# Input rows and result rows of an S4 block with an MLP: one transfer of 128 partitions, or four of 32

## The chip, the cores and the metric

The kernel runs on one core of a Trainium2 chip. The metric is the device time of one execution, in microseconds (us). A core has a matrix engine (TensorE, "PE" in the profile), a vector engine (DVE), a scalar engine (ACT), GpSimd (POOL) and SyncE (SP), which in this kernel only issues transfers. Each engine works through its own instructions strictly in order. The transfers themselves (DMAs) run on 16 DMA engines that all queues share.

## The reference, cut to what matters

2048 tokens of 512 channels, all in float32. The block is a layer norm with a scale and a shift from a conditioning vector, a long convolution over the tokens (S4), a residual addition, a second layer norm, an MLP with Mish, and a second residual addition.

```python
x = A_u                                    # (1, 2048, 512)
mod = (silu(c) @ w_mod)...                 # sa, ca, ga, sb, cb, gb
h = layernorm(x) * (1 + ca) + sa
x = x + ga * S4(h)                         # K from exp(dt*A*l), then FFT convolution, + h * Dskip
h = layernorm(x) * (1 + cb) + sb
x = x + gb * (mish(h @ w1 + b1) @ w2)      # w1 512 x 1792, w2 1792 x 512
```

## The kernel before

**Layout of the tokens.** A token number is split as 64·p + 16·a + j, with p from 0 to 31, a from 0 to 3 and j from 0 to 15. A tile of input rows holds on partition 32·a + p, for one or several j, the 512 channels of the token: four groups of 32 partitions, one for each a. In DRAM a step in p is 64 rows, a step in a is 16 rows, and n successive j are n successive rows, so that a partition's share is one stretch of n · 2 KB. The result tiles of the MLP (`ot`) have the same layout with one j.

**The head.** The first transfers on SP's queue are small parameters (`ldt`, `raw`, `ident`, `cT`, `dtap`, `hl`), then the input rows: five calls of `x_rows` in line 630 load all 2048 rows (4 MB) into the tiles `xr` in the order j = 12 to 15, 4 to 7, 8 and 9, 10 and 11, 0 to 3. Behind them on the same queue come the constants `bdk`, `bdu`, `di`, `b1`, the 2 MB table `mf` (line 694), the first four tiles of the conditioning weights `wm` (line 433), and the 2 MB table `mi` (line 698). On GpSimd's queue `sel`, `mc`, `ac` and `su` are loaded at the same time.

**Who uses the rows first.** `stats` takes mean and variance of each row: for j = 12 to 15 on ACT (`junk`, lines 680 and 684), for the others on DVE (`bst`, line 674). `norm` (line 498) then normalizes all 16 row tiles, and `ua` (line 505) sends them through TensorE as the first step of the convolution's transform. Meanwhile `params` prepares the exponents of the convolution kernel on DVE and ACT (`raw`, an arctangent among it, lines 281 and 291), and TensorE builds the angles (`psel`, line 307, `pang`, line 346) and the conditioning (`pmodr`, line 440, which reads `wm`). ACT, DVE and PE each have an order in which these two strands are interleaved, and a wait in one strand holds up the other.

**The middle.** Four blocks of 128 channels go through kernel generation, transform, product and inverse in a software pipeline whose order comes from the table `ORDER` and the priorities in `PRI` and `PRI0`; the framework makes the fixed order of each engine's instructions and all the waits from these. In this stage `x_rows` is called with a block number `b` (line 602): it loads 128 of the 512 channels and already makes four transfers of 32 partitions, 64 KB each. The sum of input and convolution is stored to DRAM as `x2d`.

**The MLP.** Four token tiles `tt` of 512 tokens, each with 14 blocks `f` of the hidden layer. `mm1` makes one hidden block (12 matmuls into a bank `pm`), ACT applies Mish, and `mm2`, two blocks behind, adds it to the four output banks `PO[tt][q]` (12 matmuls `po`). The six PSUM banks rotate, so that the banks of the next token tile come free when `fin_q` has read those of the last one. `fin_q` (line 895) does this for each q: DVE multiplies the bank by the gate (line 903, the step that frees the bank), adds the residual `xr` or `xf` (line 904), and SP stores the tile `ot` (line 905). `ot` has two buffers, so the multiplication for q = 2 waits until the store of q = 0 has landed, and the one for q = 3 until the store of q = 1 has. Between the stores SP's queue holds the loads of `xr` from `x2d` (line 899, four for each q).

Of the kernel before, what the change touches and what calls it, by code (L numbers as in the profile page):

```python
# [18 lines left out]
P = 128  # L19
D = 512  # L20
# [93 lines left out]
def s4_block(ctx, tc, io, out):  # L114
    nc = tc.nc
# [32 lines left out]
    def view(src, offset, ap):  # L148
        return bass.AP(tensor=src.tensor, offset=src.offset + offset, ap=ap)
# [35 lines left out]

    def x_rows(dst, j0, n, b=None):
        w = D if b is None else P
        if b is None:
            nc.sync.dma_start(dst, view(io["A_u"], j0 * D, [[16 * D, 4], [64 * D, 32], [1, n * D]]))  # L189
            return  # L190
        for a in range(4):
            nc.sync.dma_start(dst[32 * a:32 * a + 32], view(io["A_u"], (16 * a + j0) * D + b * P,
                                                            [[64 * D, 32], [D, n], [1, P]]))

    bdk = cst.tile([P, 256], F32, name="bdk")
    bdu = cst.tile([P, 64], F32, name="bdu")
# [392 lines left out]
    def s_xp(y):  # L589
        b, hf, j4 = y // 8, y % 8 // 4, y % 4  # L590
        if hf == 0:
            return
        if b < NB - 1:
            t = cv.tile([P, 4, P], F32, tag="xp", name=f"xp{b}{j4}", bufs=2)
        elif j4 == 0:
            t = LNX[0][:, b]
        else:
            if j4 == 1:
                XP[b] = sl8(f"xp{b}").rearrange("p (q j d) -> p q j d", q=4, j=4)
            t = XP[b][:, j4]  # L600
        XP[b, j4] = t
        x_rows(t, 4 * j4, 4, b)
# [23 lines left out]
    for j0, t in ((12, xr3), (4, xr01[:, 4:8]),  # L626
                  *((j, cv.tile([P, 2, D], F32, tag="x4", name=f"xr{j}", bufs=3)) for j in (8, 10)),
                  (0, xr01[:, 0:4])):
        n = t.shape[1]
        x_rows(t, j0, n)  # L630
        XR[j0:j0 + n] = [t[:, q, :] for q in range(n)]
# [263 lines left out]
    def fin_q(tt, q, x=None):  # L895
        if x is None:
            x = MW["wr"].tile([P, NB, P], F32, tag=("yt", "q1")[q % 2], name="xr", bufs=1)
            for b in range(NB):
                nc.sync.dma_start(x[:, b], x2d[b][:, 4 * tt + q, :])
        else:  # L900
            x = x[:, :, q, :]
        o = mp.tile([P, NB, P], F32, tag="ot", name="ot")
        V.tensor_mul(o.rearrange("p b d -> p (b d)"), PO[tt][q], gbb)  # L903
        V.tensor_add(o, o, x)
        nc.sync.dma_start(view(out, (4 * tt + q) * D, [[16 * D, 4], [64 * D, 32], [1, D]]),
                          o.rearrange("p b d -> p (b d)"))

    tables("mish")
    seq = [(tt, f) for tt in range(4) for f in range(FB)]
    for n, (tt, f) in enumerate(seq):  # L910
        mm1(tt, f)
        if tt == 0:
            load_w2(f)
        if tt + 1 < 4:
            if f == 7:
                ln_load(tt + 1)
            if f == 11:
                ln_stats(tt + 1, range(NB))
                ln_norm(tt + 1)
            if f == 13:  # L920
                ln_t(tt + 1)
        if n == 3:
            gb_row()
        if n >= LAG:
            pt, pf = seq[n - LAG]
            mm2(pt, pf)
            if pf == FB - 1:
                for q in range(4):
                    fin_q(pt, q)
    xl = fin_load(3)  # L930
    for q in range(4):
        for f in range(FB - LAG, FB):
            mm2(3, f, (q,))
        fin_q(3, q, xl)
# [37 lines left out]
```

## Time and profile before

| | us |
|---|---|
| median of 3 runs | 782.93 |
| lowest and highest of them | 779.67, 785.41 |
| the profiled execution's own time | 784.37 |
| its span, from the first to the last recorded event | 782.6 |
| TensorE busy in it | 663.6 (85%) |
| DVE, ACT, GpSimd busy | 432.4 (55%), 339.0 (43%), 51.7 (7%) |
| mean TensorE clock granted | 0.938 |

The busy shares are means over stages that are limited by different things. The first 80 us, in which TensorE works little, and the hand-over from one token tile to the next in the MLP are read by their own waits and from the chain that ended last. In the rows of a timeline the first number is the start, the second the duration, and a bracket at the end tells how long the engine had been idle and what released it. In the rows by windows the last two numbers are the mean busy share of the 16 DMA engines and the rate that they moved.

### The profile page before, as it was taken

How to read it: one execution, taken by the hardware profiler on the slowest of the kernel's cores; microseconds unless marked ns; L12 is line 12 of the kernel's file. 1: busy time of each engine (PE TensorE's matmuls, PEld its weight loads, DVE VectorE, ACT ScalarE, POOL GpSimd, SP SyncE). 2: the span in 40 equal slices, each digit the busy share in tenths (PEclk: the TensorE clock that was granted, in tenths of full speed). 3: DMA queues.
4: the chain of work that ended last, by engine and by line, in shares of the span. 5: the costliest groups of instructions: out<-in, count | busy, mean ns of one | idle time of the engine just before them, and what ended most of it. 6: DMA issues, size and time to landing. Idle time of an engine off the chain costs nothing.

```text
span 782.6 us, 14045 instructions
## 1 busy us (share of the span) xinstructions
PE 663.6 (85%) x5696; PEld 510.8 (65%) x5696; DVE 432.4 (55%) x900; ACT 339.0 (43%) x529; POOL 51.7 (7%) x111
## 2 busy tenths in 40 slices
PE   0427897799999999999855799997999899989991
PEld 0214355467888878888631588886888688868881
DVE  6319885597999989995742891182113311331112
ACT  2543468555787686765520542241223222322220
POOL 1000142050206020000000000000000000000000
PEclk9957789899999999999986999998999999999997
DMA  5247488653326553565866730013001210010001
GB/s 156 109 131 295 122 189 194 189 131 101 84 67 154 156 153 95 137 185 175 249 200 168 236 95 1 0 55 103 5 1 54 67 41 0 1 54 27 1 1 54
DMA packets 97228, 82.91 MB, mean 106 GB/s; under 512 B 10376, under 2 KB 78732, under 8 KB 96524
## 3 DMA queue, kind: packets, MB, share of 16 engines
q1 hardware_dynamic: 90444, 78.14, 34.6%
q0 software_dynamic: 6720, 3.87, 2.6%
q8 instruction: 45, 0.74, 0.4%
q14 instruction: 19, 0.16, 0.1%
HBM read 54.72 MB, written 25.17 MB: 102 GB/s over the span
## 4 chain that ended last, share of the span: by engine, by line
PE 69%; DMA 10%; SPq 8%; DVE 6%; ACT 4%; issue 1%; POOL 0%; DVEq 0%; ACTq 0%; POOLq 0%
PE pm L867 18%; PE po L885 17%; PE pkg L392 4%; PE pub L525 4%; PE pang L346 4%; DMA out<-ot 4%; PE pkb L525 3%; PE pka L409 3%; SPq L189 3%; PE pib L574 3%; PE pang L350 3%; SPq L694 2%; PE pmodr L440 2%; PE pt L566 2%; DMA wm<-in_w_mod 1%
## 5 line engine op out<-in xcount | busy, mean ns | idle before, releaser
L867 PE MATMUL pm<-hh,w1h 128*128 128x512 f32 x448 | 141.1, 396 | 7.0 <-DVE ot L903 4.7
L874 DVE TENSOR_TENSOR mal<-mh,mah 128x512 fp32r<-128x512 f32 x56 | 38.6, 691 | 171.3 <-ACT mah L873 170.8
L138 ACT ACTIVATE mh<-pm,b 128x512 f32<-128x512 f32 x56 | 38.5, 690 | 216.0 <-PE pm L867 216.0
L867 PEld LDWEIGHTS pm<-hh,w1h 128*128 128x128 f32 x448 | 85.4, 192 | 26.9 <-DVE ot L903 5.1
L885 PE MATMUL po<-w2h,mah 128*128 128x512 f32 x224 | 88.2, 394 | 5.6 <-DVE ot L903 5.6
L867 PE MATMUL pm<-hh,w1l 128*128 128x512 f32 x224 | 88.3, 394 | 0.0
L885 PE MATMUL po<-w2h,mal 128*128 128x512 f32 x224 | 87.9, 393 | 0.0
L885 PE MATMUL po<-w2l,mah 128*128 128x512 f32 x224 | 87.8, 392 | 0.0
L559 DVE TENSOR_TENSOR q<-pkb,ug 128x512 f32<-128x512 f32 x64 | 41.2, 685 | 19.4 <-PE pkb L525 19.2
L885 PEld LDWEIGHTS po<-w2h,mah 128*128 128x128 f32 x224 | 42.1, 188 | 14.7 <-DVE ot L903 6.5
L867 PEld LDWEIGHTS pm<-hh,w1l 128*128 128x128 f32 x224 | 42.9, 191 | 8.9
L357 ACT ACTIVATE ec<-pang 128x1024 f32<-128x1024 f32 x32 | 32.8, 1026 | 35.1 <-PE pang L346 28.7
L885 PEld LDWEIGHTS po<-w2h,mal 128*128 128x128 f32 x224 | 42.2, 188 | 8.9 <-DVE mal L874 0.3
L885 PEld LDWEIGHTS po<-w2l,mah 128*128 128x128 f32 x224 | 42.1, 188 | 8.4
L377 DVE TENSOR_TENSOR ec<-ec,m 128x1024 f32<-128x1024 f32 x32 | 39.0, 1220 | 9.2 <-ACT ec L138 9.0
L350 PE MATMUL pang<-rnd,oneb 128*128 128x512 bf16 x128 | 41.7, 410 | 0.0
L367 DVE TENSOR_TENSOR m<-co 128x1024 f32<-128x1024 f32 x32 | 39.0, 1220 | 1.3 <-ACT co L138 0.9
L346 PE MATMUL pang<-nac,s 128*128 128x256 f32 x128 | 39.4, 390 | 0.0
L409 PE MATMUL pka<-bdk,ks 128*64 128x128 f32 x512 | 38.0, 280 | 1.3 <-DVE ks L398 1.3
L381 DVE TENSOR_TENSOR ec<-ec,m 128x1024 f32<-128x1024 f32 x32 | 39.0, 1218 | 0.1
L392 PE MATMUL pkg<-ec 128*32 128x64 f32 x2048 | 38.9, 226 | 0.0
L525 PE MATMUL pub<-mf,gu 128*128 128x128 f32 x256 | 37.1, 288 | 1.6 <-DMA gu<-ud 1.6
(165 smaller groups left out, 1117.9 us busy)
## 6 DMA issues: line engine op xcount, KB each, us to landing
ud<-us SPq DMA_DIRECT2D x64, 128.0 KB, 2.8
gu<-ud SPq DMA_DIRECT2D x32, 256.0 KB, 3.6
zd<-z SPq DMA_DIRECT2D x32, 256.0 KB, 3.8
zt<-zd SPq DMA_DIRECT2D x32, 256.0 KB, 5.9
wm<-in_w_mod SPq DMA_DIRECT2D x24, 256.0 KB, 5.6
out<-ot SPq DMA_DIRECT2D x16, 256.0 KB
xp<-in_A_u SPq DMA_DIRECT2D x60, 64.0 KB, 2.3
x2d<-xp SPq DMA_DIRECT2D x15, 256.0 KB, 2.4
```

The source lines that it names most:

```text
L346: T.matmul(p[:, e, 256 * q:256 * q + 256], S12[b, 2 * q + c // 4][:, e, :], w[:, 32 * o:32 * o + 256], start=(w is ac and q == 0), stop=(w ...
L350: T.matmul(p[:, e, :], oneb.to_broadcast([P, P]), rnd[:, z:z + 1].to_broadcast([P, 512]), start=False, stop=False, skip_group_check=True)
L367: V.tensor_mul(m2.rearrange("p d (a b) -> p d a b", a=8), co[:, :, 12:20, None].to_broadcast([P, 16, 8, 8]), co[:, :, None, 20:28].to_broa ...
L377: V.tensor_mul(ec[:, :, :, 32:64], ec[:, :, :, 95:63:-1], m2[:, None, :, 0:32].to_broadcast([P, 2, 16, 32]))
L381: V.tensor_mul(ec[:, :, :, 0:32], ec[:, :, :, 0:32], m1[:, None].to_broadcast([P, 2, 16, 32]))
L392: T.matmul(o, ec[:, z, e, 0:32], ec[:, z, e, 32:96], start=(z == 0), stop=(z == 1))
L409: T.matmul(pv[64 * cc:64 * cc + 64, :, o:o + 4], KS[k][:, 64 * m:64 * m + 64], bdk[:, 128 * cc:128 * cc + 128], start=True, stop=True)
L525: T.matmul(pv[:, :, r, :], lh(r), mf[:, 4 * s + r, :].rearrange("p (c s) -> p c s", c=2), start=not started, stop=True, skip_group_check=s ...
L559: V.tensor_mul(q, kv[:, c, :, None, :].to_broadcast([P, 4, 2, 64]), ug)
L867: T.matmul(p, w1[wi][:, k, fs], hh[:, hi, k, :], start=(n == 0), stop=(n == 3 * KB - 1))
L874: V.tensor_sub(a[1], h, a[0])
L885: T.matmul(PO[tt][q], a[ai][:, P * q:P * q + P], w2[wi][:, f, :], start=(f == 0 and n == 0), stop=(f == FB - 1 and n == 2))
```

## The change

`x_rows` without a block number no longer makes one transfer over four groups of 32 partitions, but takes the loop that the calls with a block number took already: four transfers, one for each group a, with the 32 partitions as the outermost dimension on both sides. The five loads of input rows (three of 1 MB, two of 512 KB) become twenty (twelve of 256 KB, eight of 128 KB). The store of each result tile (256 KB) becomes four of 64 KB: sixteen stores become sixty-four. The bytes and the stretches in DRAM stay the same, 2 KB to 8 KB each, and so do the tiles and all the arithmetic.

```diff
     def x_rows(dst, j0, n, b=None):
         w = D if b is None else P
-        if b is None:
-            nc.sync.dma_start(dst, view(io["A_u"], j0 * D, [[16 * D, 4], [64 * D, 32], [1, n * D]]))
-            return
         for a in range(4):
-            nc.sync.dma_start(dst[32 * a:32 * a + 32], view(io["A_u"], (16 * a + j0) * D + b * P,
-                                                            [[64 * D, 32], [D, n], [1, P]]))
+            nc.sync.dma_start(dst[32 * a:32 * a + 32], view(io["A_u"], (16 * a + j0) * D + (0 if b is None else b * P),
+                                                            [[64 * D, 32], [D, n], [1, w]]))
...
         V.tensor_add(o, o, x)
-        nc.sync.dma_start(view(out, (4 * tt + q) * D, [[16 * D, 4], [64 * D, 32], [1, D]]),
-                          o.rearrange("p b d -> p (b d)"))
+        for a in range(4):
+            nc.sync.dma_start(view(out, (16 * a + 4 * tt + q) * D, [[64 * D, 32], [1, D]]),
+                              o[32 * a:32 * a + 32].rearrange("p b d -> p (b d)"))
```

## Prediction

> **What bounds the kernel now.** I read the page first, then the rates by windows of 5 us in the head, the chain that ended last, and the timelines of the engines around the two places that the change touches.
>
> ```profile
> span 782.6 us, 14045 instructions
> ...
> PE 69%; DMA 10%; SPq 8%; DVE 6%; ACT 4%; issue 1%; POOL 0%; DVEq 0%; ACTq 0%; POOLq 0%
> ...
> out<-ot SPq DMA_DIRECT2D x16, 256.0 KB
> xp<-in_A_u SPq DMA_DIRECT2D x60, 64.0 KB, 2.3
> x2d<-xp SPq DMA_DIRECT2D x15, 256.0 KB, 2.4
> ```
>
> TensorE carries 69% of the chain that ended last, but transfers and SP's queue carry 18%, some 140 us. The change only touches SP's queue and what travels on it, so the question is which pieces of those 18% are input rows or result stores. The last two rows are prices for later: a load of 64 KB in 32 partitions lands 2.3 us after its issue, a store of 256 KB in 128 partitions in 2.4 us.
>
> The head by windows (the last two numbers are the busy share of the 16 DMA engines and GB/s):
>
> ```profile
> 5.00:10.00 5.00, 0.00 (x0) 0.00 (x0) 2.67 (x19) 0.00 (x0) 0.00 (x0) 1.00 0.99 282
> 10.00:15.00 5.00, 0.00 (x0) 0.00 (x0) 4.00 (x20) 3.39 (x5) 0.00 (x0) 1.00 0.38 95
> 15.00:20.00 5.00, 0.00 (x0) 0.00 (x0) 3.16 (x11) 0.00 (x0) 0.00 (x0) 1.00 0.25 79
> 20.00:25.00 5.00, 0.00 (x0) 0.00 (x0) 0.00 (x0) 0.06 (x1) 0.00 (x0) 1.00 0.25 105
> 45.00:50.00 5.00, 3.83 (x12) 2.62 (x12) 0.00 (x0) 2.11 (x4) 0.00 (x0) 0.50 0.25 105
> 60.00:65.00 5.00, 1.51 (x5) 0.54 (x6) 5.00 (x15) 0.00 (x0) 0.00 (x0) 0.50 1.04 419
> ```
>
> From 15 us to 50 us the share is 0.25, which is 4 of 16 engines, at 105 GB/s. From 60 us on all 16 engines together move 419 GB/s. The only large transfers in flight in between are the input rows. SP shows the same from its side, in the chain:
>
> ```profile
> 4.47 0.60 SPq L189
> ...
> 8.45 13.10 SPq L189
> ...
> 39.20 15.99 SPq L694
> ...
> 55.23 8.12 DMA wm<-in_w_mod
> ```
>
> The row loads are issued from 4.47 us on, but an issue then hangs for 13.1 us, and that of `mf` (line 694) for 16 us until 55.19. Only then do the first weights `wm` go out. Three engines wait for this:
>
> ```profile
> 24.95 0.63 ACT L680 ACTIVATE junk<-xr 128x512 f32<-128x512 f32 x1 [10.89 <-DMA xr<-in_A_u]
> ```
> ```profile
> 27.41 0.29 DVE L291 SCALAR_TENSOR_TENSOR raw<-raw 128x128 f32<-128x128 f32 x1 [9.25 <-ACT raw L138]
> ...
> 55.03 1.29 DVE L674 BATCH_NORM_STATS2 bst<-xr 128x6 f32<-128x512 f32 x2 [20.29 <-DMA xr<-in_A_u]
> ```
> ```profile
> 29.44 2.12 PE L307 MATMUL psel<-pk,sel 32*128 32x384 f32 x8 [29.44 <-DVE pk L247]
> ...
> 63.49 3.81 PE L440 MATMUL pmodr<-wm,sc 128*32 128x512 f32 x8 [14.51 <-DMA wm<-in_w_mod]
> ```
>
> ACT stands 10.9 us for the first megabyte. The arctangent behind it in ACT's order holds DVE 9.25 us, and DVE holds PE's first matmul. Then DVE stands 20.3 us for the last rows, and PE 14.5 us for `wm`, which are behind the rows on SP's queue.
>
> The same width shows in the stores. In the chain and in the timelines of the MLP:
>
> ```profile
> 526.73 6.79 DMA out<-ot
> ...
> 606.99 0.69 PE po L885 x3
> ...
> 609.73 6.72 DMA out<-ot
> ...
> 692.77 6.71 DMA out<-ot
> ...
> 765.33 7.24 DMA out<-ot
> ```
> ```profile
> 534.36 1.22 PE L867 MATMUL pm<-hh,w1h 128*128 128x512 f32 x2 [4.70 <-DVE ot L903]
> ...
> 617.29 0.63 PE L885 MATMUL po<-w2h,mah 128*128 128x512 f32 x1 [2.82 <-DVE ot L903]
> ...
> 700.31 0.50 PE L885 MATMUL po<-w2h,mah 128*128 128x512 f32 x1 [2.80 <-DVE ot L903]
> ```
>
> A store of `ot` needs 6.7 us where the page has 2.4 us for another store of the same 256 KB. At each of the three hand-overs the third multiplication waits for it, and PE for the multiplication.
>
> **The change part by part: can the pieces use more engines?** The case has pieces of 32 partitions already, the `xp` loads. Here eight of them are issued back to back, with nothing else issued meanwhile:
>
> ```profile
> 337.63 3.67 SPq L192 DMA_DIRECT2D xp<-in_A_u  x8
> ```
> ```profile
> 339.60:340.60 1.00, 1.00 (x59) 0.88 (x61) 0.97 (x3) 1.00 (x2) 0.00 (x0) 1.00 0.50 140
> ```
>
> The share is 0.50, twice what four engines could show, and 64 KB per 0.46 us (3.67 / 8) is 142 GB/s, so SP's issuing was the limit and not the engines. The width of such a piece is thus at least 8 engines; I take 16, and keep 8 as the other end. [...]
>
> **Head.** SP issues 20 loads instead of 5: 4.47 + 20 x 0.46 = 13.7 us, and the queue no longer stands still, so the issuing isn't the limit. Rows: 4.19 MB at 419 GB/s is 10.0 us (20 us with 8 engines). The other traffic of the head is through at about 11 us by the shares 0.99 and 0.38. If the rows had to wait for all of it, the first megabyte would be there at 11 + 2.5 = 13.5 us and the last at 21 us, plus 2 for landing.
>
> ACT's idle time began at 24.95 - 10.89 = 14.1 us: its wait of 10.9 us goes. DVE was done with what it had at 27.41 - 9.25 = 18.2 us, so line 291 and PE's `psel` come 9.2 us earlier, and with them the whole PE block that ended at 63.49 - 14.51 = 49.0 us: now 39.8 us. Next on PE are the eight `pmodr`, which need `wm`. Behind the rows come 0.2 MB of small constants, the 2.1 MB of `mf` and 1.05 MB of `wm`, 3.35 MB / 419 = 8 us: there at 23 + 8 = 31 us, 9 us before PE wants them (with 8 engines for the rows about 40 us, just in time). So `pmodr` starts at 39.8 instead of 63.5 us, 23.7 us earlier. DVE's wait for the last rows ended at 55.0; its queue reaches that point at 34.7 - 9.2 = 25.5 us, after the rows: 29.5 us earlier. PE gains less, and DVE later waits for PE's products, so PE's 23.7 us count. What is late next is PE's own first block, from 20 to 40 us. Nothing behind it is tied to a clock time, so the 23.7 us stay to the end. Bounds: 9.2 if only ACT's wait went, 29.5 if PE were no limit.
>
> **Hand-overs.** A store becomes four issues. At 0.46 us each the last starts 1.4 us after the first and lands 2.4 us later: 3.8 us instead of 6.7, a gain of 2.9. With the issue at 0.58 us it would be 2.6. PE's three waits of 4.70, 2.82 and 2.80 us shrink to 1.8, 0 and 0: 8.5 us. Something else goes with them. After the waits PE was slow:
>
> ```profile
> 534.36 5.16 PE pm L867 x12
> ...
> 542.28 2.72 PE pm L867 x12
> ```
> ```profile
> 617.29 1.49 PE po L885 x3
> 618.78 3.81 PE pm L867 x12
> ```
> ```profile
> 534.00:536.00 2.00, 1.64 (x4) 1.35 (x5) 0.91 (x2) 0.00 (x0) 0.00 (x0) 0.50 0.47 144
> ```
>
> Twelve matmuls that otherwise take 2.72 us took 5.16 after the first wait (2.4 lost); after the second, three took 1.49 instead of 0.69 and twelve 3.81 (1.9 lost). The window says why: the granted clock there is 0.50 (third number from the end). I take these 4.3 us as gained too, as waits of under 2 us should not lower the clock where the one of 2.82 lost less than the one of 4.70; at the other end they stay. Against this stands what is queued behind the longer issue: SP has two `xr` loads between the stores, and the store of q = 1 follows 1.4 us later than it could. It lands 3.8 us after its first issue all the same, where now it shares four engines with its predecessor, so the multiplication for q = 3 doesn't become the wait. Sum: 12.8 us, between 6 (8.5 with a longer issue and no clock gain) and 14.
>
> **End.** Here nothing covers the stores:
>
> ```profile
> 770.09 0.69 DVE L903 TENSOR_TENSOR ot<-po,gbb 128x512 f32<-128x512 f32 x1 [4.79 <-DMA out<-ot]
> ```
> ```profile
> 774.10 0.54 SPq L905 DMA_DIRECT2D out<-ot  x1
> ```
>
> The multiplication for q = 2 waits 4.79 us for the store of q = 0, and after the last issue at 774.10 another 6.7 us of landing follow, going by the other stores. With pieces the third multiplication comes about 2 us earlier. The last store follows its predecessor's four issues and lands at about 776 instead of 781: 4.9 us, between 3.5 and 5.5.
>
> **Sum.** 23.7 + 12.8 + 4.9 = 41.4 us off the profiled execution's own 784.4 gives 743.0. That execution lies 1.4 us above the median of the three, inside their spread of 5.7, so I leave 743.
>
> **The rivals.** *The head gives less* (0.18). Something between 9.2 and 23.7 us, if `wm` are late. For it: SP's queue can stand for older transfers, as this row of the waits has it (5.7 us in 5 waits), though line 899 needs nothing of the stores:
>
> ```profile
> SPq L899 <- DMA out<-ot: 5.7, 5, 1.7
> ```
>
> If SP went in groups of eight, each lasting the 8.1 us of `wm`, its 36 issues up to `wm` would take 36 us, and `wm` would be there at 4.5 + 36 + 8 = 48: `pmodr` 15 us earlier. Against it: pieces land in about 2.3 us. Times 752 to 757. A different interleaving of the engines' orders, made anew with 63 more instructions, would fall here too.
>
> *The pieces travel no wider than the whole and only add issues* (0.04, slower). Then a store lands 3 x 0.46 = 1.4 us later, at three hand-overs and twice at the end (6.9 us), and the head is 15 x 0.46 = 6.9 us later: 784.4 + 13.8 = 798. It decides from the point where a piece lands later than 6.7 - 1.4 = 5.3 us after its issue; the share of 0.50 and the 2.3 us speak against it. [...]
>
> *No change* (0.04): wider stores eaten by issues, and PE's head bound by something that I don't see.
>
> **How the numbers follow.** Forecast 0.74, the others 0.18, 0.04, 0.04. The forecast's own bounds are 784.4 - 29.5 - 14 - 5.5 = 735 and 784.4 - 20 - 6 - 3.5 = 755; a head of only 9 us, with the middle of the other terms, gives 760. I take 735 to 762. Everything faster than 775 us is faster by over 1%, about what can be told from no change: 0.92. Within 1% 0.04, slower 0.04.
>
> **What would show it.** The DMA share from 12 to 20 us near 0.9 instead of 0.25; no issue of a row load over 3 us; ACT's `junk` and DVE's `bst` without a wait of 10 and 20 us; `pmodr` at about 40 us; stores of about 4 us in the chain; PE's waits at the hand-overs under 2 us. The forecast is wrong if the share stays at 0.25, or if PE's start moves while `pmodr` doesn't.

## The result, and the profile after

| | us |
|---|---|
| changed kernel, median of 4 runs (lowest, highest) | 758.0 (755.87, 760.26) |
| kernel before, median of 4 runs beside it | 784.17 |
| ratio, 95% interval | 0.967, 0.961 to 0.973: faster |
| profiled execution of the changed kernel, its span | 760.26, 758.5 |

26 us less. That is faster, inside the stated range (735 to 762) and above the forecast of 743; 41 us were forecast. From the page of the changed kernel, the span, the shares of the chain that ended last, and the row of the stores:

```profile
span 758.5 us, 14126 instructions
...
PE 76%; DMA 7%; DVE 6%; ACT 6%; SPq 3%; issue 2%; POOL 0%; DVEq 0%; ACTq 0%; POOLq 0%
...
out<-ot SPq DMA_DIRECT2D x64, 64.0 KB, 1.7
```

Transfers and SP's queue hold 10% of the chain instead of 18%, and a piece of a store lands 1.7 us after its issue, where the whole store took 6.7. Where the time was won is seen from where the stages begin. These are the matmuls `pm`, whose first start is the beginning of the MLP (the last numbers before the semicolon are the first and the last start), before and then after:

```profile
L867 PE MATMUL pm<-hh,w1h x448: 387/389/793, 437.2 to 757.8; 128*128 128x512 f32 x150
```
```profile
L864 PE MATMUL pm<-hh,w1h x448: 387/389/504, 435.5 to 741.7; 128*128 128x512 f32 x150
```

All that lies ahead of the MLP gained 1.7 us (437.2 to 435.5), where 23.7 were forecast. From the first to the last `pm` it is 306.2 us instead of 320.6: 14.4 us gained, forecast 12.8. From the last `pm` to the end of the span 16.8 us instead of 24.8: 8.0 gained, forecast 4.9. The sum is the 24.1 us by which the span is shorter. The MLP did a little more than it was to do; the head's gain is missing.

It isn't missing at its start. The windows of the changed kernel (DMA share and GB/s last), and its SP queue:

```profile
15.00:20.00 5.00, 0.51 (x3) 0.32 (x3) 5.00 (x21) 1.59 (x2) 0.00 (x0) 1.00 0.99 219
20.00:25.00 5.00, 4.87 (x20) 3.39 (x19) 4.93 (x24) 3.48 (x11) 0.00 (x0) 1.00 1.07 248
```
```profile
4.39 20.03 SPq L189 DMA_DIRECT2D xr<-in_A_u  x20
...
31.74 2.45 SPq L430 DMA_DIRECT2D wm<-in_w_mod  x4
```

The share is 1.0 instead of 0.25: all 16 engines. `wm` go out at 31.7 instead of 55.2 us. But on DVE and PE things stand in another place than before (line numbers behind the change are 2 or 3 lower, so 671 is the former 674):

```profile
53.85 1.28 DVE L671 BATCH_NORM_STATS2 bst<-xr 128x6 f32<-128x512 f32 x2
...
65.16 7.62 DVE L495 TENSOR_SCALAR xr<-xr,mv,rstd 128x512 f32<-128x512 f32 x16
72.70 0.15 DVE L395 TENSOR_TENSOR ks<-ks,dtap 128x4 f32<-128x4 f32 x1
```
```profile
47.98 1.69 PE L437 MATMUL pmodr<-wm,sc 128*32 128x512 f32 x4
...
72.91 0.69 PE L406 MATMUL pka<-bdk,ks 128*64 128x128 f32 x2 [16.75 <-DVE ks L395]
```

SP has issued the last of these rows by 24.4 us (4.39 + 20.03), but DVE takes their first statistics at 53.85 us. Before, it had them behind the preparation of the first exponents; now they stand behind the exponents' products (`ec`, `m`) of three steps and the first product of the fourth, and the whole block of statistics and normalization stands ahead of `ks`, for which PE is idle for 16.75 us. In the two built programs 153 of DVE's 900 places hold another instruction than before, 57 of ACT's 521 and 191 of PE's 4008. Nearly all of these are in the head, the rest at the hand-overs.

### The profile page after: what moved, and what is told of

The parts are those of the page before. It is cut to its first block, busy times and chain, and to the rows that moved or that the text cites. A ratio compares the mean times of both kernels' runs of the same rounds, so it can differ in the third digit from the quotient of the medians.

```text
span 758.5 us, 14126 instructions
## 1 busy us (share of the span) xinstructions
PE 662.4 (87%) x5696; PEld 510.4 (67%) x5696; DVE 434.8 (57%) x900; ACT 339.2 (45%) x529; POOL 51.7 (7%) x111
## 4 chain that ended last, share of the span: by engine, by line
PE 76%; DMA 7%; DVE 6%; ACT 6%; SPq 3%; issue 2%; POOL 0%; DVEq 0%; ACTq 0%; POOLq 0%
PE pm L864 18%; PE po L882 18%; PE pang L343 4%; PE pub L522 4%; PE pkg L389 4%; PE pka L406 4%; PE pang L347 4%; PE pkb L522 4%; PE pib L571 4%; PE pt L563 2%; PE pmodr L437 2%; ACT ec L354 2%; PE pua L502 1%; DMA raw<-in_par 1%; PE pia L609 1%
## 5 line engine op out<-in xcount | busy, mean ns | idle before, releaser
L864 PE MATMUL pm<-hh,w1h 128*128 128x512 f32 x448 | 138.6, 390 | 2.2 <-ACT hh L775 1.2
L864 PEld LDWEIGHTS pm<-hh,w1h 128*128 128x128 f32 x448 | 83.7, 188 | 21.6 <-ACT hh L775 2.1
L374 DVE TENSOR_TENSOR ec<-ec,m 128x1024 f32<-128x1024 f32 x32 | 39.1, 1221 | 20.2 <-ACT ec L138 19.9
L406 PEld LDWEIGHTS pka<-bdk,ks 128*64 128x64 f32 x512 | 29.3, 139 | 24.5 <-DVE ks L395 18.4
L343 PE MATMUL pang<-ac,s 128*128 128x256 f32 x128 | 31.0, 325 | 13.2 <-ACT ec L138 13.0
L571 PE MATMUL pib<-yt,mi 128*128 128x128 f32 x256 | 36.6, 288 | 4.5 <-ACT yt L565 4.5
```

The source lines that it names most:

```text
L343: T.matmul(p[:, e, 256 * q:256 * q + 256], S12[b, 2 * q + c // 4][:, e, :], w[:, 32 * o:32 * o + 256], start=(w is ac and q == 0), stop=(w ...
L374: V.tensor_mul(ec[:, :, :, 32:64], ec[:, :, :, 95:63:-1], m2[:, None, :, 0:32].to_broadcast([P, 2, 16, 32]))
L406: T.matmul(pv[64 * cc:64 * cc + 64, :, o:o + 4], KS[k][:, 64 * m:64 * m + 64], bdk[:, 128 * cc:128 * cc + 128], start=True, stop=True)
L571: T.matmul(p[:, P * r:P * r + P], mi[:, 4 * s + r, :], YT[v][:, r, :], start=True, stop=True)
L864: T.matmul(p, w1[wi][:, k, fs], hh[:, hi, k, :], start=(n == 0), stop=(n == 3 * KB - 1))
```

## The experiments

All ratios are to runs of the kernel before on the same chip, with 95% intervals. Theory 1: the wider loads are worth the forecast 23.7 us, and the order of the engines that the framework made anew spent them. Theory 2: they are worth little in themselves.

**The two parts by themselves (e1, e2).** e1 has the edit of `x_rows` alone, e2 that of `fin_q` alone, as in the diff of the change.

> The input rows in pieces, the stores of ot whole. The prediction's sum put the head at 23.7 us: 760 us. Theory 1 (the gain of the wider loads is spent on the new order of DVE, ACT and PE in the head): the first pm comes at about 435.5 us as in the changed kernel, against 437.2 before, so about 782 us. Theory 2 (the wider loads are worth little by themselves, something in the middle takes up whatever the head gains): about 782 us too. This run only divides the gain between the two parts of the change.

> The stores of ot in pieces, the input rows whole. The prediction's sum put hand-overs and end at 17.7 us: 766 us. From the trace of the changed kernel (from the first pm to the end 323.0 us against 345.4) it should be 22.4 us less than before: about 762 us. If the MLP's gain depended on the head, more than 770.

e1: 780.1 us, ratio 0.994 (0.991 to 0.996). e2: 765.2 us, ratio 0.973 (0.968 to 0.977), 21 us. The stores carry nearly the whole result; the rows gave 5 us by the ratio. PE's row for `ks` in e1, then the MLP in e2:

```profile
75.11 0.69 PE L419 MATMUL pka<-bdk,ks 128*64 128x128 f32 x2 [16.65 <-DVE ks L408]
```
```profile
L877 PE MATMUL pm<-hh,w1h x448: 387/389/793, 440.9 to 747.7; 128*128 128x512 f32 x150
```

In e1 PE waits 16.65 us for `ks`, as in the changed kernel. In e2 there is no such wait, and its `pmodr` still start at 64.9 us, with 25.7 us of waits for `wm` in all (before the change 63.5 and 26.8): the new order in the head comes from `x_rows`. The gain in the MLP comes from the stores: from the first to the last `pm` it is 306.8 us in e2, in e1 320.3.

**Loads and order apart (e3, e4).** The framework's order can be held fixed by ordering edges without semaphores between the instructions of one engine. In e3 and in e4 the program of the other form is traced first, and its order, kept for each engine in `how["order"]`, is imposed:

```diff
+    for e, order in how["order"].items():
+        gs = groups[e]
...
+        seq = [i for k in order for i in gs[k]]
+        for a, b in zip(seq, seq[1:]):
+            tc.add_manual_dep(b, a.name, no, reason="order of the other kernel")
```

> Both parts of the change, but DVE, ACT, PE, GpSimd and SP hold their instructions in the order of the kernel before (the pieces of a transfer stand where the whole one stood). Theory 1: the head gains the predicted 23.7 us, pmodr starts at about 40 us, the first pub at about 125 us, and the time is 784 - 23.7 - 22.4 = 738 us. Theory 2: the time stays at 755 to 760 us, with the first pub at 140 us or later.

> Neither part of the change, but all engines hold their instructions in the order of the changed kernel. Theory 1: the new order costs; its pmodr waits for wm at about 63 us instead of 48 us, and what follows comes some 13 us later than in the changed kernel's head: about 795 us, slower than before. Theory 2 (the order matters little): 784 us within 4.

e3: 742.7 us, ratio 0.946 (0.941 to 0.950), 43 us faster than the kernel before and 22.5 us faster than e2. Its waypoints, from the views of the tiles `pmodr`, `pub` and `pm`:

```profile
L450 PE MATMUL pmodr<-wm,sc x48: 592/616/1061, 40.7 to 158.8; 128*32 128x512 f32 x48
```
```profile
L535 PE MATMUL pub<-mf,gu x256: 275/275/377, 124.5 to 381.8; 128*128 128x128 f32 x128
```
```profile
L877 PE MATMUL pm<-hh,w1h x448: 387/389/501, 414.0 to 720.1; 128*128 128x512 f32 x150
```

`pmodr` starts at 40.7 us (forecast 39.8), and the MLP begins 437.2 - 414.0 = 23.2 us earlier (forecast 23.7). The order is the only difference from the changed kernel. Theory 2 falls. The profiled execution is the fastest of e3's four, but the 22.5 us to e2, by the medians, tell the same.

e4 contradicts the form in which I had put theory 1. It is not slower than before but faster: 771.4 us, ratio 0.979 (0.974 to 0.985).

```profile
L877 PE MATMUL pm<-hh,w1h x448: 387/389/628, 433.8 to 748.2; 128*128 128x512 f32 x150
```
```profile
58.96 1.29 DVE L684 BATCH_NORM_STATS2 bst<-xr 128x6 f32<-128x512 f32 x2 [2.83 <-DMA xr<-in_A_u]
```

With the narrow loads the MLP begins at 433.8 us in the new order, 3.4 us before the old order's 437.2. That is no more than e2, with the old order in the head, lies behind it (440.9), so the two orders are about equal there. DVE asks for the rows only at 56 us and so waits 2.83 us for them instead of 20.29. The rest of the 9.6 us that the profiled span gains lies in the MLP, where the new order has PE wait 6.0 us in all for the multiplications at the hand-overs, before 10.3. So the new order isn't a bad one. It is one for late rows, and under it early rows are of no use: 433.8 us with narrow loads, 435.5 with wide ones. Under the old order it is 437.2 and 414.0.

**Width or number (e5).** The twenty loads are cut by columns instead, in e3's order:

```diff
+            m = n * D // 4
+            f = dst.rearrange("p j d -> p (j d)")
+            for c in range(4):
+                nc.sync.dma_start(f[:, m * c:m * c + m], view(io["A_u"], j0 * D + m * c, [[16 * D, 4], [64 * D, 32], [1, m]]))
```

> As e3 (stores of ot in pieces, order of the kernel before), but the twenty loads of input rows are cut the other way: four transfers of a quarter of the columns each, with the four token groups outermost and 128 partitions in each. The number of transfers and their bytes are those of e3. If the width comes from 32 being outermost: the DMA share stays at 0.25 in the head, pmodr starts at about 64 us, and the time is that of e2, about 765 us. If it comes from the number of transfers in flight: as e3, 743 us.

762.3 us, ratio 0.967 (0.961 to 0.974), e2's within the intervals. The window of the head and PE's wait:

```profile
20.00:25.00 5.00, 1.84 (x8) 1.43 (x8) 3.87 (x21) 4.15 (x10) 0.00 (x0) 1.00 0.26 102
```
```profile
62.94 3.44 PE L450 MATMUL pmodr<-wm,sc 128*32 128x512 f32 x8 [20.67 <-DMA wm<-in_w_mod]
```

Twenty transfers with the four groups outermost still have a quarter of the full share (0.26, where e3's twenty show 1.01 to 1.07). Here it is the outermost dimension and not the number. The cut by columns also makes the stretches in DRAM shorter (1 to 2 KB instead of 4 to 8) and covers 128 partitions, but neither explains the share: the kernel before had 0.25 with the long stretches, and e10 below has 1.02 to 1.05 with 128 partitions.

**Which engine's order (e6 to e9).** Both parts of the change, with only the engines named held in the old order; the list of engines is the whole edit:

```diff
-ENGINES = ("PE", "DVE", "Activation", "Pool", "SP")
+ENGINES = ("DVE",)                     # e7: Activation, PE   e8: SP   e9: Activation, DVE
```

> Both parts of the change; only DVE holds the order of the kernel before, the other engines get whatever order the framework makes with that. If the cost of the new order lies in DVE's block of statistics and normalization ahead of the first ks (PE stands 16.75 us for it): 743 us within 5, and PE has no wait of over 5 us for ks. If it lies in the orders of PE, ACT or SP: 755 to 760 us.

> Both parts of the change; ACT and PE hold the order of the kernel before, DVE and SP get a new one. If DVE's order is what costs: 755 to 762 us, with a wait of PE for ks of some 15 us. If ACT's or PE's does: about 743 us.

> Both parts of the change; only SP holds the order of the kernel before, so that mi and the second wm go out in their old places (at about 32 and 42 us instead of 54 us). If the late issue of mi and wm is what costs: about 743 us. If DVE's order does: 755 to 760 us.

> Both parts of the change; DVE and ACT hold the order of the kernel before, PE and SP get whatever order the framework makes with that. In e6 DVE alone stood 16.6 us for ACT's junk, which ACT's new order puts behind the first ec. If the cost of the new order is the place of the row statistics on these two engines: as e3, 0.945 of the time before, about 744 us. If PE's or SP's order has a share: between 750 and 760 us.

e6: 754.9 us, ratio 0.958 (0.952 to 0.965). e7: 759.7 us, 0.963 (0.957 to 0.969). e8: 758.6 us, 0.961 (0.954 to 0.968). e7 and e8 stay at the changed kernel's time. In both PE waits for `ks`, in e7 and then e8:

```profile
71.53 0.69 PE L419 MATMUL pka<-bdk,ks 128*64 128x128 f32 x2 [20.19 <-DVE ks L408]
```
```profile
72.85 0.69 PE L419 MATMUL pka<-bdk,ks 128*64 128x128 f32 x2 [15.84 <-DVE ks L408]
```

In e6 that wait is gone, but the time isn't e3's, and its expectation (743 within 5) was missed. DVE's own row tells why:

```profile
38.55 0.17 DVE L691 TENSOR_SCALAR nmr<-sq 128x4 f32<-128x4 f32 x1 [16.59 <-ACT junk L690]
```

The rows' statistics are shared between DVE and ACT. ACT's new order has its part (`junk`) behind the first sines, and DVE in the old order stands 16.59 us for it. With both engines in the old order, e9 gives 745.0 us, ratio 0.947 (0.944 to 0.950), as e3.

```profile
L880 PE MATMUL pm<-hh,w1h x448: 387/389/504, 419.2 to 725.4; 128*128 128x512 f32 x150
```

The loss lies in the orders of DVE and ACT. That it is the place of the row statistics in them is read from the two waits of 16.75 and 16.59 us; no run moved the statistics alone. The orders of PE and SP, which the framework then made itself, cost nothing that the ratios can tell apart, though in the profiled executions e9's MLP begins at 419.2 us and e3's at 414.0, so up to 5 us may be theirs.

**The rate of the rows (e10).** The rows moved at 219 to 263 GB/s with all engines busy, not at the 419 that I had put in. e10 loads them in five transfers with 128 partitions outermost, in e3's order. It puts other tokens' rows on the partitions than the later steps assume, so it doesn't compute the block's result; the work is the same.

```diff
+        if b is None and how["head"] == "straight":
+            nc.sync.dma_start(dst, view(io["A_u"], j0 * D, [[16 * D, P], [1, n * D]]))
+            return
```

> As e3, but the input rows are loaded in five transfers of 128 partitions with the partitions outermost, 16 rows apart: all 16 engines without cutting. Each partition gets rows of another token than it should, the arithmetic is the same. The pieces of 32 partitions moved 219 to 263 GB/s at a DMA share of 1.0, where 419 GB/s had been forecast. If the 32 partitions of a piece are what slows the engines: the rows move at about 400 GB/s here and are in by 20 us. If it is the rows themselves (their stretches in DRAM): 220 to 260 GB/s here too. Either way PE's first block ends at about 40 us and the time is e3's within 4 us.

737.7 us, ratio 0.937 (0.935 to 0.940). e3's window, then two of e10:

```profile
15.00:20.00 5.00, 0.00 (x0) 0.00 (x0) 3.07 (x13) 3.25 (x8) 0.00 (x0) 1.00 1.01 229
```
```profile
10.00:15.00 5.00, 0.00 (x0) 0.00 (x0) 3.86 (x20) 2.80 (x4) 0.00 (x0) 1.00 1.05 404
15.00:20.00 5.00, 0.00 (x0) 0.00 (x0) 5.00 (x21) 4.37 (x10) 0.00 (x0) 1.00 1.02 419
```

With 128 partitions outermost in one transfer the rows moved at 404 to 419 GB/s, with stretches in DRAM of the same length. So the length of the stretches isn't what slows the pieces; their 32 partitions most likely are. e10 also has five transfers for twenty and a step of 16 rows in DRAM for 64, and no run parts these. For the time it matters little: `pmodr` starts at 40.1 us in e10 and at 40.7 us in e3, and the profiled spans are 737.2 and 736.8 us. The median is 5 us lower than e3's, where at most 4 had been expected; it is from another set of runs, and that difference is left open.

## Why the prediction was right, and where it was wrong

**What bounds the head: right.** The row loads ran on 4 of 16 engines because the four groups were outermost, and in pieces of 32 partitions they run on 16. e5, with e3's number, bytes and order of transfers, shows the first (share 0.26), the changed kernel the second (share 1.0). That a piece gets 16 engines was my choice between 8 and 16: the kernel before showed 0.50 for pieces (the `xp` loads), and only the changed kernel showed 1.0.

**The rate of the rows: mis-sized, without effect.** Working with 419 GB/s, I had the last rows in at 21 to 23 us. The pieces move 219 to 263 GB/s, and in e3 DVE still waits 3.22 us for them, until 29.69 us. The 9 us to spare before `pmodr` took this up. With the rate the issuing was off too. SP's twenty issues end at 24.4 us, not at 13.7, since SP waits for earlier transfers to land, 7.9 us of it for earlier pieces:

```profile
SPq L189 <- DMA xr<-in_A_u: 7.9, 12, 1.4
```

e10's 404 to 419 GB/s belong to one transfer with 128 partitions outermost; the whole transfers of the kernel before, also over 128 partitions but with the four groups outermost, moved 105 GB/s. Why pieces of 32 partitions stay at 219 to 263 GB/s isn't shown.

**PE's 23.7 us "stay to the end": the step that failed.** PE's waypoints came true in e3 (40.7 against 39.8 us for `pmodr`, 23.2 against 23.7 us at the MLP), where the order is that of the trace I had read. I had worked the whole head out in that order. That the edit adds 63 instructions for SP, and that the order is made anew with them, stood only as one sentence at the first rival, priced at 752 to 757 us. It was the main term: 23.7 forecast, 1.7 measured at the MLP's start of the changed kernel, and 23.2 with the order held. Held on DVE and ACT alone, the old order brings the time back to 745 us (e9). The first rival's own mechanism, SP standing for older transfers until `wm` are late, didn't decide: SP did stand 7.9 us for earlier pieces, but in the changed kernel `wm` are issued by 34.2 us, and its `pmodr` at 48 us stand behind more of PE's own angles than before.

That the time still fell inside the range is partly luck. The head's 1.7 us lie even below the bound of 9.2 that I had given it; with the forecast 12.8 and 4.9 us for the rest the time would have been 765, outside. And the range reached 762 only by a head of 9 us, while the sum for its 755 uses one of 20 us, for which I showed no row. Of the signs I had listed, the DMA share, the short issues and the missing waits of ACT and DVE all came. Only `pmodr` at 48 us instead of 40 hinted at the loss, and no sign looked behind it.

**Hand-overs: right, 14.4 us against 12.8.** The row for the tile `ot` of the changed kernel has, of the three PE waits of 10.3 us, this left:

```profile
  PE pm L864: 0.8, 1
```

The forecast left 1.8 us of wait. The piece lands in 1.7 us, where 2.4 had been taken. Most of the lost matmul time went with the waits: after the first hand-over twelve `pm` take 3.02 us instead of 5.16.

```profile
528.83 3.02 PE pm L864 x12
```

The order has no visible part in this: e3, in the old one, has 306.1 us from the first to the last `pm`, the changed kernel 306.2.

**End: right in kind, 8.0 us against 4.9.** DVE's last two waits for a store are 1.81 and 0.45 us instead of 4.79 and 1.15. The last rows of DVE before, then after:

```profile
772.66 0.69 DVE L903 TENSOR_TENSOR ot<-po,gbb 128x512 f32<-128x512 f32 x1 [1.15 <-DMA out<-ot]
773.39 0.69 DVE L904 TENSOR_TENSOR ot<-ot,xf 128x512 f32<-128x512 f32 x1
```
```profile
750.97 0.69 DVE L900 TENSOR_TENSOR ot<-po,gbb 128x512 f32<-128x512 f32 x1 [1.81 <-DMA out<-ot]
...
752.84 0.69 DVE L900 TENSOR_TENSOR ot<-po,gbb 128x512 f32<-128x512 f32 x1 [0.45 <-DMA out<-ot]
753.57 0.69 DVE L901 TENSOR_TENSOR ot<-ot,xf 128x512 f32<-128x512 f32 x1
```

The third multiplication gained 3.0 us (about 2 forecast), the fourth another 0.7 (nothing forecast), and the last store the rest: from the end of the last addition to the end of the span it is 4.2 us instead of 8.5, 4.3 gained where 2.9 were forecast. Part of the excess is the landing of a piece, 0.7 us shorter than the 2.4 taken.

**The slower rival: wrong.** It had a piece landing later than 5.3 us after its issue; the measured median is 1.7 us. And the pieces did travel wider than the whole: the share is 1.0 instead of 0.25. They only fell short of the rate of a transfer with 128 partitions outermost, 219 to 263 GB/s against e10's 404 to 419.

What isn't shown is why the framework put the statistics later. That it takes twenty transfers on one queue to be done later than five is a guess; no run looked into its reckoning.

## What to carry to other kernels

If a transfer is slow, look at its outermost dimension and at the DMA share while it runs alone. Here it was 0.25, that of 4 of 16 engines, at 105 GB/s with four groups outermost; the same bytes cut into pieces of 32 partitions had 1.0 and 219 to 263 GB/s, cut by columns still 0.26. If a framework makes the order of the engines, an edit to the transfers is an edit to that order as well: compare the orders first, and hold the old one fixed once, so that the worth of the transfer and the worth of the order can be told apart. The faster input paid only under the order that asked for it early: the MLP began at 414.0 instead of 437.2 us in the old order, at 435.5 instead of 433.8 in the new one.

## What the runs showed of the hardware that was not expected

All 16 engines were busy (share 1.0) at 219 to 263 GB/s when each transfer covered 32 partitions, and moved 404 to 419 GB/s with 128 partitions, with the same stretches in DRAM. A full share was thus not a full rate: at share 0.25 the rows had moved 105 GB/s, which promised four times that. And the small stores were quick: 64 KB from 32 partitions landed 1.7 us after the issue (median of 64), 256 KB with the four groups outermost took 6.7 us, at a share of 0.26 (768 to 770 us in the kernel before).
